# Opening of a fused attention and two-layer feed-forward kernel: pair sums, key copies and three divisions on GpSimd, two chunks of layer one in halves

## The chip, the cores and the metric

The kernel runs on one core of one Trainium2 chip. The metric is the device time of one execution in microseconds (us); lower is better. Work is shared out over five engines, each with its own in-order queue: TensorE (PE in the rows; PEld is its weight load), VectorE (DVE), ScalarE (ACT), GpSimd (POOL) and SyncE (SP), which here issues all DMAs. An engine that waits for a semaphore holds up everything behind the waiting instruction on its own queue.

## The reference

Block-sparse attention over two batches of 768 tokens (8 heads of 64), then two feed-forward layers over the 1536 tokens. Each query sees the 31 tokens around it and 24 summaries, one for each block of 32 tokens: the maximum of the block's keys, the mean of its values.

```python
k_sum = k.reshape(B, H, nb, block, D).max(axis=3)
v_sum = v.reshape(B, H, nb, block, D).mean(axis=3)
scores_l = scale * np.matmul(q, k.transpose(0, 1, 3, 2))
mask_l = np.abs(pos[:, None] - pos[None, :]) < window
scores_s = scale * np.einsum('bhsd,bhnd->bhsn', q, k_sum) + np.log(block)
scores_all = np.concatenate([np.where(mask_l, scores_l, -1e9), scores_s], axis=-1)
a = np.exp(scores_all - np.max(scores_all, axis=-1, keepdims=True))
a = a / (np.sum(a, axis=-1, keepdims=True) + 1e-09)
x = np.matmul(a, np.concatenate([v, v_sum], axis=2))     # then laid out as 1536 x 512
h = np.maximum(x @ w_in, 0.0);  x = h * h @ w_out        # layer one, 512 -> 2048 -> 512
h = x @ w_in2;  out = (h / (1 + np.exp(-h))) @ w_out2    # layer two
```

## The kernel before

Attention goes by 24 tiles of 64 queries, twelve for each batch. A tile's scores are, for each of four pairs of heads (hp), products of its queries with 120 columns: 96 tokens around the tile and the 24 key summaries. Layer one goes by three blocks of 512 tokens, and in each block by 16 chunks of 128 hidden units. A chunk s is one `gemm1` (12 products of 128x512, which fill one accumulator h) and one `gemm2` (12 products). All large products are split in a high and a low part, so three products stand for one.

The first block cannot begin before the first eight tiles, the **lead**, have given 512 rows of x. This is the part that is touched, in `first_block`. Its steps carry short names; of the lead, for tile g and pair hp:

- `kt`, `q`, `vr`, `vl`, `raw`: loads, in this order on SyncE. `kt` is a head pair's keys of a whole batch, `vr` a third of the batch's values, for the means (`vrows`), `vl` the values of four tiles, `raw` a packed weight chunk (`wi` or `wo`).
- `ksum` (VectorE): block maxima of the keys of one pair. `kwl` (ScalarE, 128x384) copies the token columns of four tiles into `kws`, `ksl` (VectorE, 128x96) the summaries beside them; index i is 0 for tiles 0 to 3 and 1 for tiles 4 to 7, so there are eight of each.
- `psl` (TensorE): the scores of one tile and pair, two instructions, read `kws`. `ttl` (VectorE, line 400): mask and minimum. `exl` (ScalarE, line 405): the exponential with its sum.
- `ze`, `rc`, `nt` (VectorE): the guard, the inverse and the four divisions of T. `psa`: transposes on TensorE. `a`: their copy on ScalarE. `av`: product with the values (TensorE). `xh` (ScalarE) and `xl` (VectorE) write the high and the low part of x.
- `vs` (TensorE): the block means of the values, six products of `vrows` with a matrix `share` of 1/32. `vmean` (ScalarE) copies the result, 24x2048, into `vlead` beside the values of tiles 0 to 3 (i = 0) and 4 to 7 (i = 1). `vfm` copies it to two later buffers.
- `sc`, `hi` (ScalarE), `sh`, `st2`, `lo` (VectorE): unpacking and splitting a weight chunk. `relu`, `sq`, `gh` (ScalarE), `gl` (VectorE): between `gemm1` and `gemm2`. `pss`, `ttr`, `exp` and `kwc` are the score steps of the later tiles 8 to 15, which are put in between the chunks.

What sets the order: `first_order` is a list planner. Each step has an engine, a duration, a due time and what it depends on; the planner walks a clock and hands out the steps, and the queues of ScalarE, VectorE, TensorE and SyncE follow its order as it stands (`manual_schedule`). GpSimd is not among these four: where an instruction stands on its queue is settled by the framework, not by the planner. Before, GpSimd has nothing to do in the lead but set small buffers.

Twenty idle products (`turn`, `FILL`) stand on TensorE at the very start and behind the first products of tile 3; they write to a spare accumulator.

## Time and profile before

| | us |
|---|---|
| median of 3 runs (593.97 to 595.03) | 594.18 |
| the profiled execution, its own time | 595.07 |
| its span, first to last instruction | 593.3 |
| busy in the span: PE, DVE, ACT, POOL | 584.0, 388.7, 367.1, 88.9 |
| granted TensorE clock, mean | 0.999 |

Rows of the timeline give the start, the busy time, the engine and line, the operation, what it writes and reads, and how many were merged; on VectorE and ScalarE one instruction's busy time overlaps the next one's start, so what an instruction takes of its queue is the distance of two starts. Idle time before a row stands in brackets with what ended it.

### The profile page before, as it was taken

How to read it: one execution, taken by the hardware profiler on the slowest of the kernel's cores; microseconds unless marked ns; L12 is line 12 of the kernel's file. 1: busy time of each engine (PE TensorE's matmuls, PEld its weight loads, DVE VectorE, ACT ScalarE, POOL GpSimd, SP SyncE). 2: the span in 40 equal slices, each digit the busy share in tenths (PEclk: the TensorE clock that was granted, in tenths of full speed). 3: DMA queues.
4: the chain of work that ended last, by engine and by line, in shares of the span. 5: the costliest groups of instructions: out<-in, count | busy, mean ns of one | idle time of the engine just before them, and what ended most of it. 6: DMA issues, size and time to landing. Idle time of an engine off the chain costs nothing.

```text
span 593.3 us, 9499 instructions
## 1 busy us (share of the span) xinstructions
PE 584.0 (98%) x3300; PEld 491.9 (83%) x3300; DVE 388.7 (66%) x975; ACT 367.1 (62%) x848; POOL 88.9 (15%) x93
## 2 busy tenths in 40 slices
PE   7989999999999999999999999999999999999997
PEld 6578888887887887888888898999988998889995
DVE  5989999733756665267544676777776766666542
ACT  5999998654555655375553676566656655555532
POOL 0000000012554443156333300000000000000000
PEclk9999999999999999999999999999999999999999
DMA  8999999525598888526682112242229411111102
GB/s 308 270 290 352 345 360 339 185 83 181 189 345 303 284 269 303 211 107 206 233 274 68 36 36 89 88 144 88 84 89 378 174 39 36 31 25 35 36 19 106
DMA packets 42240, 104.42 MB, mean 176 GB/s; under 512 B 4560, under 2 KB 11856, under 8 KB 42192
## 3 DMA queue, kind: packets, MB, share of 16 engines
q1 hardware_dynamic: 42192, 103.81, 51.4%
q8 instruction: 26, 0.43, 0.3%
q14 instruction: 22, 0.18, 0.1%
HBM read 78.37 MB, written 25.43 MB: 175 GB/s over the span
## 4 chain that ended last, share of the span: by engine, by line
PE 95%; ACT 2%; DMA 1%; DVE 1%; issue 0%; SPq 0%; DVEq 0%
PE acc L238 45%; PE h L238 23%; PE hx L238 11%; PE hz L238 6%; PE pss L238 4%; PE hy L238 3%; PE psa L442 2%; PE av L238 2%; DMA t_ksum<-in_kT_dram 1%; ACT T L405 1%; PE psv L238 1%; ACT vlead L242 1%; ACT a L242 0%; ACT xt L242 0%; PE idle_out L238 0%; DVE ksum L620 0%
## 5 line engine op out<-in xcount | busy, mean ns | idle before, releaser
L238 PE MATMUL acc<-wq,g 128*128 128x512 f32 x576 | 142.4, 392 | 0.0
L238 PE MATMUL h<-xt,wi 128*128 128x512 f32 x576 | 142.2, 394 | 0.0
L238 PE MATMUL acc<-g,wo 128*128 128x512 f32 x576 | 141.1, 393 | 0.0
L238 PEld LDWEIGHTS acc<-g,wo 128*128 128x128 f32 x576 | 107.1, 188 | 23.1 <-ACT xt L242 0.2
L238 PEld LDWEIGHTS h<-xt,wi 128*128 128x128 f32 x576 | 106.3, 188 | 22.9 <-issue 0.6
L238 PEld LDWEIGHTS acc<-wq,g 128*128 128x128 f32 x576 | 107.1, 188 | 19.7 <-DVE wq L246 0.2
L246 DVE TENSOR_TENSOR g<-r,g 128x512 fp32r<-128x512 f32 x48 | 38.4, 801 | 60.5 <-ACT g L242 31.0
L246 DVE TENSOR_TENSOR r_s<-v,r_s 128x256 fp32r<-128x256 f32 x48 | 20.5, 431 | 50.2 <-ACT r_s L242 50.1
L242 ACT ACTIVATE g<-s 128x384 fp32r<-128x384 f32 x64 | 33.2, 521 | 22.0 <-DVE s L246 22.0
L246 DVE TENSOR_TENSOR g<-s,g 128x384 fp32r<-128x384 f32 x64 | 35.5, 556 | 15.1 <-ACT g L242 13.2
L405 ACT ACTIVATE T<-T,m 128x120 f32<-128x120 f32 x96 | 36.7, 384 | 11.2 <-DVE m L400 11.0
L242 ACT ACTIVATE e<-hx 128x384 f32<-128x384 f32 x32 | 15.7, 492 | 43.8 <-PE hx L238 43.8
L238 PE MATMUL hx<-x_t,r_s 128*128 128x384 f32 x192 | 38.9, 337 | 0.0
L238 PEld LDWEIGHTS hx<-x_t,r_s 128*128 128x128 f32 x192 | 34.5, 188 | 2.7
L932 ACT ACTIVATE s<-e 128x384 f32<-128x384 f32 x48 | 25.2, 525 | 15.4 <-DVE e L246 15.3
L246 DVE TENSOR_TENSOR s<-e,s 128x384 f32<-128x384 f32 x48 | 26.5, 553 | 5.2 <-ACT s L932 5.2
L526 ACT ACTIVATE r<-h 128x512 f32<-128x512 f32 x16 | 9.5, 596 | 30.9 <-PE h L238 30.9
L246 POOL TENSOR_TENSOR wo<-c_wo,wo 128x512 fp32r<-128x512 f32 x16 | 26.1, 1632 | 13.1 <-ACT wo L242 12.6
L242 ACT ACTIVATE r<-u 128x256 fp32r<-128x256 f32 x48 | 19.5, 409 | 12.7 <-PE hx L238 12.7
L243 POOL COPY qd<-qr 128x256 f32<-128x256 f32 x8 | 5.8, 719 | 133.7 <-DVE z L425 125.8
L400 DVE CUSTOM_DVE_ANT_0 T<-pss,cst_sb 128x120 f32<-128x120 f32 x96 | 21.8, 274 | 4.3 <-PE pss L238 4.0
L246 POOL TENSOR_TENSOR r<-r 128x512 f32<-128x512 f32 x16 | 17.0, 1064 | 48.6 <-ACT g L531 48.6
(112 smaller groups left out, 912.0 us busy)
## 6 DMA issues: line engine op xcount, KB each, us to landing
raw_wi<-in_w_in_dram SPq DMA_DIRECT2D x16, 512.0 KB, 5.6
raw_wo<-in_w_out_dram SPq DMA_DIRECT2D x16, 512.0 KB, 5.6
raw_wp<-in_w_out_dram SPq DMA_DIRECT2D x16, 512.0 KB, 5.4
split<-wo SPq DMA_DIRECT2D x16, 512.0 KB, 3.7
raw_wj<-in_w_in_dram SPq DMA_DIRECT2D x16, 512.0 KB, 4.6
wo<-split SPq DMA_DIRECT2D x16, 512.0 KB, 3.4
c<-scr_dram SPq DMA_DIRECT2D x32, 256.0 KB, 2.6
scr_dram<-c_wo SPq DMA_DIRECT2D x16, 256.0 KB, 4.4
```

The source lines that it names most:

```text
L238: pe.matmul(o, l, r, **kw)
L242: return act.activation(out=o, in_=i, func=AF.Copy, scale=scale)
L243: return eng.tensor_copy(out=o, in_=i)
L246: return eng.tensor_tensor(out=o, in0=a, in1=b, op=op)
L400: vec.tensor_tensor_reduce(out=d["T"][:, c], in0=d["ps"][:, c], in1=cst_sb[:, kind * NK:kind * NK + NK], scale=-0.125, scalar=3.0e38, op0= ...
L405: act.activation(out=d["T"][:, c], in_=d["T"][:, c], func=AF.Exp, bias=d["m"][:, c:c + 1], scale=-1.0, accum_out=d["z"][:, c:c + 1])
L442: pe.transpose(ps[0:NK, c], d["T"][:, c], id_sb)
L526: act.activation(out=r, in_=h, func=AF.Relu)
L932: act.activation(out=s, in_=src, func=AF.Sigmoid)
```

## The change

Seven of the eight key copies `kwl` go from ScalarE to GpSimd, and so do all eight summary copies `ksl` from VectorE. The values are loaded so that a partition holds two neighbouring tokens; GpSimd adds the two (`vpair`, 128x512, three of them), and `vs` needs three products instead of six, with a `share` that VectorE now makes from the identity in the constants (`member`). Of the two copies `vmean` the second goes from ScalarE to VectorE; `vfm` goes to GpSimd. The divisions `nt` of tiles 2, 4 and 6 go from VectorE to GpSimd. The first two chunks' `gemm1` are cut in halves of 256 tokens: `half1` reads x of tiles 0 to 3 alone and stands before the last two tiles of the lead on TensorE; the second half follows when all eight are there. Planner durations and due times are changed with it (the diff shows those that come with a moved step), and the weight chunks are taken in another order.

```diff
+NHALF = 2
+NORMS = (2, 4, 6)
...
-            op("act", "kwl", (hp, i), .5, -50 + hp + 51 * i, [("kt", hp, 0)])
-            op("vec", "ksl", (hp, i), .13, -50 + hp + 48 * i, [("ksum", hp, 0)])
-    for c in range(6):
-        op("pe", "vs", c, .92, 2.7 + .1 * c, [("vr", c // 2, 0)])
+            op("pool" if i or hp else "act", "kwl", (hp, i), .5, -50 + hp + 51 * i, [("kt", hp, 0)])
+            op("pool", "ksl", (hp, i), .25, -50 + hp + 48 * i, [("ksum", hp, A)])
+    op("vec", "member", 0, .25, 1.9, [("cst", 0, 0)])
+    for c in range(3):
+        op("pool", "vpair", c, 1.07, -20, [("vr", c, 0)])
+        op("pe", "vs", c, .95, 1.6 + .01 * c, [("vpair", c, A), ("member", 0, A)])
...
-        op("vec", "nt", g, .78, due, [("rc", g, .1)])
+        op("pool" if g in NORMS else "vec", "nt", g, 1.3 if g in NORMS else .78, due, [("rc", g, .1)])
...
+        if s < NHALF:
+            op("pe", "half1", s, 1.45, due - 30, [("xl", g, A) for g in range(NGRP)] + [("lo", ("wi", s), A)])
...
-            sp.dma_start(out=t, in_=vP[0, r0:r0 + 2 * P].rearrange("(c p) d -> p c d", p=P))
+            sp.dma_start(out=t, in_=vP[0, r0:r0 + 2 * P].rearrange("(p c) d -> p c d", p=P))
...
-            copy(act, kws[i][hp // 2][:, hp % 2, :, 0:NWIN], bass.AP(w.tensor, w.offset, [w.ap[0], [QT, NGRP], w.ap[1]]))
+            copy(pool if i or hp else act, kws[i][hp // 2][:, hp % 2, :, 0:NWIN], bass.AP(w.tensor, w.offset, [w.ap[0], [QT, NGRP], w.ap[1]]))
...
-            copy(vec, kws[i][hp // 2][:, hp % 2, :, NWIN:NK], bass.AP(s.tensor, s.offset, [s.ap[0], [0, NGRP], s.ap[1]]))
+            copy(pool, kws[i][hp // 2][:, hp % 2, :, NWIN:NK], bass.AP(s.tensor, s.offset, [s.ap[0], [0, NGRP], s.ap[1]]))
...
+        def member(_):
+            n = 2 * P // KBLK
+            rows = share[:, NSUM - n:NSUM]
+            vec.tensor_reduce(out=rows, in_=id_sb.rearrange("p (n j) -> p n j", n=n), op=ALU.add, axis=AX.X)
+            vec.tensor_scalar(out=rows, in0=rows, scalar1=1.0 / KBLK, scalar2=None, op0=ALU.mult)
+
+        def vpair(c):
+            tt(pool, vrows[c][:, 0], vrows[c][:, 0], vrows[c][:, 1], ALU.add)
+
         def vs(c):
-            lo = NSUM - P // KBLK - c * (P // KBLK)
-            mm(psv[NWIN:NK], share[:, lo:lo + NSUM], vrows[c // 2][:, c % 2], start=(c == 0), stop=(c == S // P - 1))
+            lo = NSUM - (c + 1) * (2 * P // KBLK)
+            mm(psv[NWIN:NK], share[:, lo:lo + NSUM], vrows[c][:, 0], start=(c == 0), stop=(c == S // (2 * P) - 1))
 
         def vmean(i):
             means = psv[NWIN:NK]
-            copy(act, vlead[NWIN:NK, i * NGRP:i * NGRP + NGRP].rearrange("p g h d -> p g (h d)"),
+            copy(vec if i else act, vlead[NWIN:NK, i * NGRP:i * NGRP + NGRP].rearrange("p g h d -> p g (h d)"),
                  bass.AP(means.tensor, means.offset, [means.ap[0], [0, NGRP], means.ap[1]]))
 
         def vfm(i):
-            copy(act, vf[i][NWIN:NK], vlead[NWIN:NK, 0])
+            copy(pool, vf[i][NWIN:NK], vlead[NWIN:NK, 0])
...
+        def half1(s):
+            h = hs[s] = ps_h.tile([P, 512], F32, tag="h", name=f"h0_{s}")
+            gemm1(wi1[s], x, 0, 256, h[:, 0:256])
+
         def gemm1_(s):
-            h = hs[s] = ps_h.tile([P, 512], F32, tag="h", name=f"h0_{s}")
-            gemm1(wi1[s], x, 0, 512, h)
+            if s < NHALF:
+                gemm1(wi1[s], x, 256, 256, hs[s][:, 256:512])
+            else:
+                h = hs[s] = ps_h.tile([P, 512], F32, tag="h", name=f"h0_{s}")
+                gemm1(wi1[s], x, 0, 512, h)
```

How the order moves, at three places. The first is GpSimd's queue in the lead. Before, between the last small buffers and the first work of the second block (`kws` and `t_ksum` don't occur; ISA is an instruction without operands that stands once, ahead of GpSimd's first tensor-tensor operation):

```order
L597 MEMSET t_ksum_2_184 128x16
L356 MEMSET share 32x1 x4
L597 MEMSET t_ksum_3_186 128x16
L243 COPY qd_108<-qr_106 128x256
L246 ISA
L246 TENSOR_TENSOR wo_0_1847<-c_wo_0_1848,wo_0_1847 128x512
```

Now, from the third pair's keys on (`t_ksum_2` and `t_ksum_3` are the keys of pairs 2 and 3, `kws_1` the columns of both, 133 for tiles 0 to 3 and 135 for tiles 4 to 7, `vrows` the values):

```order
L250 COPY kws_1_133<-t_ksum_2_180 128x4x96
L250 COPY kws_1_135<-t_ksum_2_180 128x4x96
L250 COPY kws_1_133<-t_ksum_3_182 128x4x96
L250 COPY kws_1_135<-t_ksum_3_182 128x4x96
L253 ISA
L253 TENSOR_TENSOR vrows_191<-vrows_191 128x512
L250 COPY kws_1_133<-ksum_197 128x4x24
L250 COPY kws_1_135<-ksum_197 128x4x24
L253 TENSOR_TENSOR vrows_193<-vrows_193 128x512
L250 COPY kws_1_133<-ksum_197 128x4x24
L250 COPY kws_1_135<-ksum_197 128x4x24
L253 TENSOR_TENSOR vrows_195<-vrows_195 128x512
```

The ISA instruction has moved from the second block into the lead, and pair 2's summary copies stand behind four key copies and behind the first pair sum, pair 3's behind the second.

The second place is TensorE where layer one begins (`h_0`, `h_1` are the accumulators of the first two chunks). Before:

```order
L238 MATMUL av_549<-a_161,vlead 64x64 x8
L238 MATMUL av_561<-a_166,vlead 64x64 x8
L238 MATMUL av_572<-a_171,vlead 64x64 x8
L238 MATMUL av_584<-a_176,vlead 64x64 x8
L238 MATMUL pss_599<-kw_245,qr_107 64x120 x8
L238 MATMUL h_0_619<-xt_88,wi_462 128x512 x12
L238 MATMUL h_1_653<-xt_88,wi_638 128x512 x12
```

Now, from the product of tile 5 with its values on:

```order
L245 MATMUL av_527<-a_162,vlead 64x64 x8
L245 MATMUL h_0_539<-xt_88,wi_498 128x256 x12
L447 MATMUL psa_571<-cst_sb,T_166 120x128 x4
L447 MATMUL psa_580<-cst_sb,T_171 120x128 x4
L245 MATMUL av_594<-a_167,vlead 64x64 x8
L245 MATMUL av_607<-a_172,vlead 64x64 x8
L245 MATMUL h_1_626<-xt_88,wi_604 128x256 x12
L245 MATMUL h_0_539<-xt_88,wi_498 128x256 x12
L245 MATMUL h_1_626<-xt_88,wi_604 128x256 x12
L245 MATMUL h_2_693<-xt_88,wi_659 128x512 x12
```

A half of each of the first two chunks stands ahead of the lead's end, and the later tile's score product `pss` that stood ahead of `h_0` has gone further back.

The third place is TensorE at tile 12 (`psv` is the batch's value summaries). Before:

```order
L238 MATMUL pss_1480<-kw_1113,qr_106 64x120 x8
L238 MATMUL pss_1496<-kw_1265,qr_107 64x120 x8
L238 MATMUL acc_0_703<-g_10_1440,wo_1210 128x512 x3
L238 MATMUL acc_1_704<-g_10_1440,wo_1210 128x512 x3
L238 MATMUL acc_2_705<-g_10_1440,wo_1210 128x512 x3
L238 MATMUL acc_3_706<-g_10_1440,wo_1210 128x512 x3
L238 MATMUL h_12_1561<-xt_88,wi_1338 128x512 x12
L442 MATMUL psa_1581<-cst_sb,T_1510 120x128 x4
```

Now:

```order
L245 MATMUL pss_1522<-kw_1127,qr_106 64x120 x8
L245 MATMUL pss_1535<-kw_1266,qr_107 64x120 x8
L245 MATMUL h_12_1560<-xt_88,wi_1329 128x512 x12
L447 MATMUL psa_1596<-cst_sb,T_1547 120x128 x4
L245 MATMUL acc_0_719<-g_11_1507,wo_1354 128x512 x3
```

The `gemm2` that stood between tile 12's scores and its transposes has gone ahead of the scores.

## Rows read from the trace of the kernel before

**Rows 1.** Busy by stretch: us, PE, PEld, DVE, ACT, POOL (instructions), PEclk, DMA share, GB/s.

```profile
15.20:37.40 22.20, 19.97 (x247) 13.03 (x245) 18.74 (x105) 21.81 (x72) 0.00 (x0) 1.00 1.02 273
37.40:145.90 108.50, 108.50 (x676) 87.02 (x674) 85.79 (x253) 83.99 (x194) 3.96 (x4) 1.00 0.78 268
589.40:591.50 2.10, 0.02 (x1) 0.00 (x0) 0.69 (x1) 0.00 (x0) 0.00 (x0) 1.00 0.54 204
591.60:593.30 1.70, 0.00 (x0) 0.00 (x0) 0.00 (x0) 0.00 (x0) 0.00 (x0) 0.50 0.09 34
```

**Rows 2.** The chain that ended last, in order of time: start us, us, what.

```profile
28.99 3.63 ACT vlead L242 x2
...
36.22 1.22 PE pss L238 x16
37.44 5.67 PE h L238 x24
```

**Rows 3.** The first load of values on SyncE: duration, start, landing.

```profile
L612 SPq DMA_DIRECT2D vrows<-in_vP_dram x1: 835/835/835, 4.1 to 4.1; - x1
...
DMA to landing us min/median/max: 9.6/9.6/9.6
```

**Rows 4.** Timeline of TensorE and VectorE in the lead: products of pair 2, block means, divisions.

```profile
12.49 4.03 PE L238 MATMUL pss<-kws,qrlead 64*64 64x120 f32 x60
...
24.35 1.90 PE L238 MATMUL psv<-vrows,share 128*24 128x512 f32 x4
24.71 0.85 DVE L436 TENSOR_SCALAR T<-T,r 128x120 f32<-128x120 f32 x4
```

**Rows 5.** Timeline of GpSimd and VectorE where GpSimd first adds.

```profile
127.13 0.63 POOL L243 COPY qd<-qr 128x256 f32<-128x256 f32 x1 [125.50 <-DVE z L425]
127.31 1.10 DVE L436 TENSOR_SCALAR T<-T,r 128x120 f32<-128x120 f32 x4
132.63 1.39 POOL L246 TENSOR_TENSOR wo<-c_wo,wo 128x512 fp32r<-128x512 f32 x1 [4.87 <-ACT wo L242]
150.87 1.04 POOL L246 TENSOR_TENSOR r<-r 128x512 f32<-128x512 f32 x1 [3.77 <-ACT g L531]
```

**Rows 6.** Timeline of ScalarE in the lead.

```profile
10.49 0.51 ACT L242 ACTIVATE kws<-t_ksum 128x384 f32<-128x384 f32 x1
...
24.45 0.60 ACT L242 ACTIVATE a<-psa 120x512 f32<-120x512 f32 x1
24.95 0.39 ACT L405 ACTIVATE T<-T,m 128x120 f32<-128x120 f32 x1
25.32 0.62 ACT L242 ACTIVATE wi<-c_wi 128x512 fp32r<-128x512 f32 x1
25.84 0.38 ACT L405 ACTIVATE T<-T,m 128x120 f32<-128x120 f32 x1
32.65 0.94 ACT L242 ACTIVATE xt<-av 128x256 fp32r<-128x256 f32 x3
```

**Rows 7.** Timeline of VectorE around the start of layer one.

```profile
36.14 0.69 DVE L293 SCALAR_TENSOR_TENSOR c_wo<-c_wo,raw_wo 128x512 int32<-128x512 int32 x1
36.75 0.75 DVE L246 TENSOR_TENSOR xt<-av,xt 128x256 fp32r<-128x256 f32 x2
37.42 0.68 DVE L293 SCALAR_TENSOR_TENSOR c_wi<-c_wi,raw_wi 128x512 int32<-128x512 int32 x1
41.03 0.42 DVE L290 TENSOR_SCALAR raw_wo<-raw_wo 128x512 int32<-128x512 int32 x1
41.37 0.27 DVE L400 CUSTOM_DVE_ANT_0 T<-pss,cst_sb 128x120 f32<-128x120 f32 x1
```

**Rows 8.** Tiles 12 and 13: score products, the next keys' load and its landing.

```profile
107.17 2.18 PE L238 MATMUL pss<-kw,qr 64*64 64x120 f32 x32
108.74 0.39 SPq L366 DMA_DIRECT2D kw<-in_kW_dram  x1
DMA to landing us min/median/max: 2.8/2.8/2.8
```

More of the change, by code (lines that the diff above doesn't have):

```diff
@@ L137, in first_order @@
         op("vec", "xl", g, .36, due, [("xh", g, A)])
-    chunks = [(x, s) for s in range(NF) for x in ("wi", "wo")]
+    chunks = sorted(((x, s) for s in range(NF) for x in ("wi", "wo")), key=lambda c: c[1] + 1.5 * (c[0] == "wo"))
     for i, (x, s) in enumerate(chunks):
@@ L157, in first_order @@
         due = chunk_due(s)
-        op("pe", "gemm1", s, 2.72, due, [("xl", g, A) for g in range(NLEAD)] + [("lo", ("wi", s), A)] +
-           [("relu", s - 2, A)] * (s >= 2))
+        if s < NHALF:
+            op("pe", "half1", s, 1.45, due - 30, [("xl", g, A) for g in range(NGRP)] + [("lo", ("wi", s), A)])
+        op("pe", "gemm1", s, 1.45 if s < NHALF else 2.72, due, [("xl", g, A) for g in range(NLEAD)] + [("lo", ("wi", s), A)] +
+           [("half1", s, 0)] * (s < NHALF) + [("relu", s - 2, A)] * (s >= 2))
         op("act", "relu", s, .57, due, [("gemm1", s, M)] + [("gl", s - 2, A)] * (s >= 2))
@@ L354 @@
     pool.memset(share, 0.0)
-    for j in range(P // KBLK):
-        pool.memset(share[j * KBLK:(j + 1) * KBLK, NSUM - P // KBLK + j:NSUM - P // KBLK + j + 1], 1.0 / KBLK)
     st = {}
@@ L734, in xh @@
             x_high(g)
-        do = dict(kt=kt, q=q, cst=cst_, vr=vr, vl=vl, ksum=ksum_, kwl=kwl, ksl=ksl, vs=vs, vmean=vmean, vfm=vfm, kv=kv, kvr=kvr,
+        do = dict(kt=kt, q=q, cst=cst_, vr=vr, vl=vl, ksum=ksum_, kwl=kwl, ksl=ksl, member=member, vpair=vpair, vs=vs, vmean=vmean, vfm=vfm, kv=kv, kvr=kvr,
                   vend=vend, vendc=vendc, vfc=vfc, kw=kw_load, qr=q_load, vf=v_load, kwc=k_sums,
                   pss=scores, ttr=minima, exp=exps, ze=guard, rc=inverse, psl=psl, ttl=lambda a: minimum(*a),
-                  exl=lambda a: exponential(*a), nt=lambda g: norm(g, vec),
+                  exl=lambda a: exponential(*a), nt=lambda g: norm(g, pool if g in NORMS else vec),
                   psa=transposes, a=a_copy, av=products, xh=xh, xl=x_low, raw=raw, sc=sc,
                   sh=lambda xs: dec_low(name(xs)),
-                  st2=lambda xs: dec_join(name(xs), cs[xs]), scr=scr_, hi=hi, lo=lo, gemm1=gemm1_, relu=relu, sq=sq, gh=gh,
+                  st2=lambda xs: dec_join(name(xs), cs[xs]), scr=scr_, hi=hi, lo=lo, half1=half1, gemm1=gemm1_, relu=relu, sq=sq, gh=gh,
                   gl=gl, gemm2=gemm2_)
```

21 lines of the change are left out of this document (11 added, 10 removed).

## The prediction

> **What bounds the kernel now.** I first read the busy time by stretch. From 37.4 us on, TensorE is busy in all of the 108.50 us of the first stretch after the lead, at the full clock, while VectorE and ScalarE are at some 80%; its last product ends at 589.4 [rows 1]. So the end is set by two numbers: when layer one starts, and how much TensorE work is left then. In the 22.2 us before, ScalarE is busy for 21.81, TensorE for 19.97, VectorE for 18.74, GpSimd not at all [rows 1]: the lead is bound by ScalarE, with 0.4 us left over. The chain of waits says the same: it runs through the two copies `vmean` on ScalarE (3.63 us, so 1.8 each), then 1.22 us of the score products `pss`, then the first two chunks `gemm1`, 5.67 us together, 2.8 each or 2.72 without their gap [rows 2]. An idea that takes 3 us of copies from ScalarE therefore aims at the right engine. What is to be settled is what the lead waits for afterwards.
>
> **The start of pair 2 (a new wait).** GpSimd's queue is not in the planner's order. In it the summary copies of pair 2 stand behind pair sum 0, which needs the first values. These were issued at 4.1 and landed 9.6 us later, at 13.7 [rows 3]. Before, nothing waited for them this early: pair 2's products began at 12.49 [rows 4]. Now: pair sum 0 starts at 13.7 and takes 1.04 to 1.39 (GpSimd's two additions of 128x512); I take 1.1, nearer to the second, which is a steady one, than to the first one after an ISA instruction [rows 5]. So 14.8. The two summary copies of 96 elements each are bounded by GpSimd's copy of 256 elements in 0.63 [rows 5]: 0.24 each in proportion, hardly under 0.13 (the planner's figure for VectorE). The first must end and be seen by TensorE, then the products run: 15.2, for 15.0 to 15.6. That is 2.7 us later than before, and since all three engines take their instructions in order, the other tiles' steps stand behind it. ScalarE starts again about 0.7 us later (two products, the mask), at 15.9.
>
> GpSimd's four key copies of pairs 2 and 3 stand ahead of pair sum 0. ScalarE could copy pair 2's first at 10.49 without waiting [rows 6], so the keys were there. At 0.63 (the 256 elements) to 0.95 (1.5 times that) they take 2.5 to 3.8 us, and end between 13.0 and 14.3; the wait for the values covers them at 0.8 each (13.7), and at the upper end they add 0.6.
>
> **ScalarE and VectorE from there.** ScalarE then has 26 of its 32 exponentials (six of pairs 0 and 1 stand ahead in its queue) by 0.38 (the distance of two starts is 0.37 without a neighbour's wait), that is 9.9; six copies `a` by 0.50, 3.0; one `vmean`, 1.8; one `sc` and one `hi`, 1.1 (0.52 for a `hi`); six `xh` by 0.28 to 0.31, 1.7 [rows 2, 6]. The sum is 17.5; with the same 0.4 of gaps as before the last exponential ends at 33.8. The seven key copies and a `vmean` are gone from it, 0.51 and 1.8 each by row [rows 2, 6], and the wait has eaten what that brought.
>
> VectorE is next. Behind the last exponential it has guard and inverse (0.25) and tile 7's divisions, 0.85 by row [rows 4]: 34.9. Then ten steps stand in its queue ahead of the last `xl`, or are it: one `sh` 0.34, two `st2` 1.22, two `sh` 0.68, a small copy 0.13, two `lo` 1.2, two `xl` 0.68, durations by the distances of starts (`st2` 36.14 to 36.75, `xl` 0.67 for two, `sh` 41.03 to 41.37) [rows 7]; 4.25 in all, so 39.15, and the second halves begin at **39.3**. By ScalarE alone (tile 7's transposes, copy, products, `xh`) it would be 37.9. The lead's end was 37.44: **+1.86**.
>
> **The halves.** A half costs 1.36. Both first halves stand ahead of the lead's end, at about 31.5 and 38.0, where TensorE has room: its lead work between 15.2 and 39.3 is some 17.7 of 24.1 us. So 2.72 us of layer one are done when the second halves start: **-2.72**. If the second of them found no gap, half of this would go. Of two moved products, the `pss` of 1.22 us [rows 2], which stood ahead of layer one, now runs behind: **+1.22**, since TensorE is full there.
>
> **Tile 12.** TensorE now runs into `psa` of tile 12 with one `gemm1` between scores and transposes, where a `gemm2` stood too. The scores end at about 108.3 before, the keys' load follows at 108.74 and lands 2.8 later [rows 8], then copy and divisions, so about 4.3 us from the scores' end (X) in the worst case, against 3.8 of cover: **+0.3**, bounds 0 and 0.8.
>
> **The clock.** While pair 2 is late, TensorE has little to do for 3 to 4 us. In the trace the granted clock was 1.00 (2.4 GHz) up to 591.5 and 0.50 (1.2 GHz) from 591.6 on, with TensorE idle since 589.4 [rows 1]. If it falls here, the products that ScalarE waits for first, 4.03 us for 60 or 0.067 each [rows 4], take twice that: eight of them add 0.5. I take **+0.2**, bounds 0 and 0.6.
>
> **Costed at nothing.** The divisions on GpSimd: 1.0 to 1.2 by its rows for 512 elements [rows 5], up to 2.1 hidden, since tile 6's scores end four exponentials (1.5 us) ahead of tile 7's and VectorE's own took 0.85; without the cover +0.6. `vs`: three products fewer of 0.47 each (1.90 for four) [rows 4], in TensorE's idle time. The second `vmean` on VectorE: up to 2.7 (2048 elements at `xl`'s 0.335 for 256 [rows 7]), beside ScalarE's exponentials; it would cost as much if `av` of tile 4 came to wait for it, but several tiles' work lies ahead. `vfm`, `member`, the small buffers: nobody waits.
>
> **The sum.** +1.86 - 2.72 + 1.22 + 0.3 + 0.2 = +0.86, say +0.9. The profiled execution took 595.07, so 595.97; it is 0.89 above the median of 594.18, so the forecast is **595.1**. What a measurement of this kernel can tell from no change is about 0.2%, 1.2 us: up to 593.0 is faster, from 595.4 slower. The forecast lies inside, near the upper edge.
>
> **Rivals.**
> (a) *The lead ends earlier than I walk it.* VectorE's ten steps need not stand in a row: those of the weights may run in its waits while ScalarE is the slower. Then the second halves start at ScalarE's 37.9, 1.4 us earlier: 593.7. Without the terms of the clock and of tile 12: 593.2. If the values, whose pieces in DRAM are now two tokens long and not one, land 1 us earlier, 592.3. For it: ScalarE, not VectorE, was the full engine [rows 1]. Against: `st2` and `xl` were close together at the lead's end before [rows 7]. Chance 0.33, of which 0.24 under 593.0.
>
> (b) *GpSimd's first addition starts late.* In front of it stands an ISA instruction without operands, now in the lead. GpSimd was idle for 4.87 us ahead of its first addition; the trace puts the end of that down to ScalarE's copy of `wo` [rows 5]. So what ISA costs by itself is between 0 and 4.87. Before pair sum 0 GpSimd has up to 1.1 us of spare time if its key copies are quick; a cost above that delays everything behind. 2.5 us would give +1.4, 596.5; 4.87 would move pair sum 0 from 12.6 to 17.5, +3.8, 598.9. This is the case that ends clearly slower; it decides from 1.1 us up. I give it 0.13, since the row has another reason for the wait.
> The Trainium skill, page "GPSIMD Engine Reference", section 2.1 "Instruction dispatch", says that the first call to a freshly loaded GpSimd function costs about 6 us that no instruction shows. By it pair sum 0 would come near 18.6 and the time near 600, an estimate from that page. The trace's 4.87 us speaks against so much, if that load happens here at all.
>
> (c) *GpSimd and VectorE slow each other.* A group of four divisions on VectorE took 0.85 alone [rows 4] and 1.10 where GpSimd's copy ran beside it [rows 5]. GpSimd now has some 7 us of work in the second part of the lead; if a third of it meets VectorE's long operations at this rate, 0.29 us for each us, with VectorE setting the end, and GpSimd's summary copies and divisions stretched as well, that is about +1.0: 596.1. Chance 0.12.
> The Trainium skill, page "Perfetto Trace Analysis", section "Optimizing Scalar/DVE Operations", says that the two share a read port, so that moving work from one to the other might not help. By that rule the copies `ksl` and the divisions bring VectorE less than their time; the trace agrees, by the 1.10 against 0.85.
>
> **How the numbers follow.** The forecast's own case has 0.42: 0.27 within 0.2%, and 0.15 above it, when the tile 12 and clock terms or the key copies come out at their upper ends (+0.5, +0.4, +0.6). Rival (a) has 0.24 faster and 0.09 same, (b) 0.13 and (c) 0.12 slower. Together: faster 0.24, same 0.36, slower 0.40. The range goes from (a) with all its parts, 592.3, to just under (b) at its upper end, 598.4.
>
> **What would show it.** In the trace after: pair sum 0 starts at 13.7, straight after its load (at 17.5 in case (b), with an idle GpSimd and landed values); the first product of pair 2 at 15.2; ScalarE idle before 15.9; the first halves at about 31.5 and 38.0 and the second from 39.3 (37.9 in (a)); a gap of 0.3 on TensorE at tile 12; the granted clock below 1.00 or not around 15 us; divisions of 1.1 and over on VectorE beside GpSimd's work (c). The forecast is wrong if pair 2 starts before 14.5, or if the second halves start outside 38.5 to 40.

## The result: slower by 6.2 us

| | before | after |
|---|---|---|
| median of four runs, us | 594.44 (593.97 to 595.03) | 600.88 (599.96 to 601.19) |
| profiled execution, its own time and span, us | 595.07, 593.3 | 601.19, 599.3 |
| granted TensorE clock, mean | 0.999 | 0.991 |

The ratio is 1.0105, with an interval of 1.0088 to 1.0123: 6.2 us of 594.4, 5.2 to 7.3. The forecast was 595.1, and the time lies above its range.

TensorE's timeline of the changed kernel in the lead (start us, busy us, engine, line, operation, what it writes and reads, shape, count, and in brackets the idle time before and what ended it) shows where it is late:

```profile
14.31 4.72 PE L245 MATMUL pss<-kws,qrlead 64*64 64x120 f32 x44 [3.13 <-POOL kws L250]
19.52 2.58 PE L245 MATMUL pss<-kws,qrlead 64*64 64x120 f32 x36 [0.49 <-DVE m L405]
22.04 0.65 PE L447 MATMUL psa<-cst_sb,T 128*120 128x128 f32 x4
...
31.80 1.62 PE L245 MATMUL av<-a,vlead 120*64 120x64 f32 x48 [1.83 <-ACT vlead L249]
...
36.13 1.70 PE L245 MATMUL h<-xt,wi 128*128 128x256 f32 x12
38.43 0.33 PE L447 MATMUL psa<-cst_sb,T 128*120 128x128 f32 x1 [0.60 <-POOL T L441]
...
43.06 2.13 PE L245 MATMUL h<-xt,wi 128*128 128x256 f32 x12
```

Pair 2 begins at 14.31 (12.49 before, [rows 4]), the first half at 36.13, the other at 43.06. That one finds no room: behind it the second halves begin at 43.06 + 2.13 = 45.19, where `gemm1` before began at 37.44 [rows 2]. From there on nothing changes any more. By stretch (us, PE busy, instructions, PEclk, DMA share, GB/s), answers of the changed kernel, those of the first block for TensorE alone, show the clock and that TensorE is full afterwards:

```profile
13.00:14.00 1.00, 0.00 (x0) 0.66 1.05 418
14.00:20.00 6.00, 5.20 (x50) 0.50 1.06 258
20.00:22.00 2.00, 2.00 (x34) 0.96 1.05 226
...
42.00:44.00 2.00, 2.00 (x26) 0.50 0.78 186
```

```profile
46.00:150.00 104.00, 104.00 (x677) 84.22 (x676) 81.71 (x246) 78.90 (x186) 3.93 (x4) 1.00 0.76 262
```

So the forecast's own sum, made with the measured start, comes out: 45.19 - 37.44 = 7.75, less 2.72 for the halves, plus 1.22 for the moved `pss`, is 6.25; the two profiled executions lie 6.12 apart. There is no gap at tile 12 (104.00 busy of 104.00). Everything that went wrong is in one term, the start of the second halves: 45.19 and not 39.3.

ScalarE's timeline of the changed kernel has these rows with an idle time ahead between its restart and the last exponential; the last row here is that exponential:

```profile
15.37 0.40 ACT L410 ACTIVATE T<-T,m 128x120 f32<-128x120 f32 x1 [4.01 <-DVE m L405]
...
20.56 0.39 ACT L410 ACTIVATE T<-T,m 128x120 f32<-128x120 f32 x1 [0.66 <-DVE m L405]
...
22.73 0.60 ACT L249 ACTIVATE a<-psa 120x512 f32<-120x512 f32 x1 [1.68 <-PE psa L447]
...
29.87 1.87 ACT L249 ACTIVATE vlead<-psv 24x2048 f32<-24x2048 f32 x1 [2.33 <-DVE vlead L250]
...
38.04 0.38 ACT L410 ACTIVATE T<-T,m 128x120 f32<-128x120 f32 x1
```

It ends at 38.42, where the forecast had 33.8, although it restarted at 15.37 and not at 15.9. The three idle times make 4.67 us; the forecast had allowed 0.4. VectorE's timeline of the changed kernel has its copy of the value means, tile 7's divisions, and the end of its work for the lead:

```profile
27.54 2.30 DVE L250 COPY vlead<-psv 24x2048 f32<-24x2048 f32 x1
...
38.98 0.97 DVE L441 TENSOR_SCALAR T<-T,r 128x120 f32<-128x120 f32 x4
...
42.28 0.68 DVE L253 TENSOR_TENSOR wi<-c_wi,wi 128x512 fp32r<-128x512 f32 x1
...
43.87 0.42 DVE L253 TENSOR_TENSOR xt<-av,xt 128x256 fp32r<-128x256 f32 x1
```

GpSimd's timeline of the changed kernel:

```profile
12.79 1.26 POOL L253 TENSOR_TENSOR vrows<-vrows 128x512 f32<-128x512 f32 x1 [1.76 <-DMA vrows<-in_vP_dram]
14.00 0.47 POOL L250 COPY kws<-ksum 128x96 f32<-128x96 f32 x2
...
23.27 4.72 POOL L441 TENSOR_SCALAR T<-T,r 128x120 f32<-128x120 f32 x8 [5.87 <-DVE z L430]
...
37.79 2.30 POOL L441 TENSOR_SCALAR T<-T,r 128x120 f32<-128x120 f32 x4 [4.75 <-DVE r L433]
```

The first pair sum starts straight on its values; they landed at 12.7, a microsecond earlier than before [rows 3]. A tile's four divisions take 2.3 us on GpSimd, where the forecast had 1.0 to 1.2, up to 2.1, and 0.85 on VectorE [rows 4].

### The profile page after: what moved, and what is told of

Read it like the earlier page. It is cut to its first block, busy times and chain, and to the rows that moved or that the text cites. A ratio compares the mean times of both kernels' runs of the same rounds, so it can differ in the third digit from the quotient of the medians.

```text
span 599.3 us, 9537 instructions
## 1 busy us (share of the span) xinstructions
PE 585.7 (98%) x3318; PEld 495.4 (83%) x3318; DVE 392.4 (65%) x958; ACT 361.9 (60%) x838; POOL 105.4 (18%) x121
## 4 chain that ended last, share of the span: by engine, by line
PE 94%; ACT 2%; DMA 1%; DVE 1%; POOL 1%; SPq 1%; issue 0%; DVEq 0%; POOLq 0%
PE acc L245 44%; PE h L245 22%; PE hx L245 11%; PE hz L245 6%; PE pss L245 4%; PE hy L245 3%; PE av L245 2%; DMA vrows<-in_vP_dram 1%; PE psa L447 1%; ACT T L410 1%; ACT a L249 0%; POOL T L441 0%; DVE vlead L250 0%; ACT vlead L249 0%; SPq L605 0%; ACT xt L249 0%
## 5 line engine op out<-in xcount | busy, mean ns | idle before, releaser
L245 PE MATMUL h<-xt,wi 128*128 128x512 f32 (+1 forms) x600 | 143.2, 387 | 0.0
L245 PEld LDWEIGHTS h<-xt,wi 128*128 128x128 f32 x600 | 107.9, 189 | 22.2 <-issue 0.6
L253 DVE TENSOR_TENSOR g<-r,g 128x512 fp32r<-128x512 f32 x48 | 37.1, 774 | 59.4 <-ACT g L249 30.3
L253 POOL TENSOR_TENSOR wo<-c_wo,wo 128x512 fp32r<-128x512 f32 x16 | 27.7, 1729 | 12.6 <-ACT wo L249 12.2
L249 ACT ACTIVATE r<-u 128x256 fp32r<-128x256 f32 x48 | 19.5, 409 | 14.0 <-PE hx L245 12.7
L249 ACT ACTIVATE a<-psa 120x512 f32<-120x512 f32 x24 | 14.1, 593 | 15.9 <-PE psa L447 15.9
```

Source lines behind the costliest of these rows:

```text
L245: pe.matmul(o, l, r, **kw)
L249: return act.activation(out=o, in_=i, func=AF.Copy, scale=scale)
L253: return eng.tensor_tensor(out=o, in0=a, in1=b, op=op)
```

## Experiments

Ratios are to the kernel before, run on the same chip in the same job, with their interval; microseconds after them are the part of that ratio above 1, times 594.4. The changed kernel stands at 1.0105, +6.2. One thousandth is 0.6 us; where two intervals overlap, as they do for every single part that was taken back except the halves, the difference of the two figures is only an indication, and what the part did is read from the rows. The rows are those of one execution of a run, its figure is the median of several. In a run "in the kept order" only the engine of a step is changed and the written order is that of the kernel it starts from; "planned anew" means that the planner's input was changed too.

### One part of the change taken back

**Summary copies back on VectorE** (kept order).

```diff
-            copy(pool, kws[i][hp // 2][:, hp % 2, :, NWIN:NK], ...
+            copy(vec, kws[i][hp // 2][:, hp % 2, :, NWIN:NK], ...
```

> The eight summary copies stand on VectorE again, in the same written order; all else as in the changed kernel. Theory A (the pair sum ahead of them on GpSimd, waiting for the values until 12.79 us, starts the loss): pair 2's products begin near 12.5 instead of 14.31, TensorE's idle time there is under 2 us, the granted clock stays at or near 1.00 between 14 and 20 us, and the time falls by 2 to 3.5, to 597.4 to 598.9. Rival B (the start is caught up again, the loss is made by the bank wait and the divisions later): the start moves, the second halves still begin within 1 us of 45.2, and the time stays within 1 of 600.9.

Measured: 1.0084 (1.0061 to 1.0108), +5.0; 1.2 taken back, within the intervals. The chain did move: pair 2 begins at 12.6, the second of the first halves at 39.83 (43.06). But VectorE's last summary copy now stands beside GpSimd's pair sum, and the clock falls later instead. VectorE's timeline, then stretches (PE, PEld, DVE, ACT, POOL, PEclk, DMA share, GB/s) of this run:

```profile
12.65 0.20 DVE L250 COPY kws<-ksum 128x96 f32<-128x96 f32 x1
12.97 1.16 DVE L250 COPY kws<-ksum 128x96 f32<-128x96 f32 x1
```

```profile
38.00:40.00 2.00, 2.00 (x33) 1.88 (x34) 2.00 (x6) 1.79 (x5) 0.00 (x0) 0.50 0.56 106
```

The same copy takes 0.20 and 1.16 us. Theory A holds for the mechanism; its size came out under the expected 2 to 3.5.

**Value means in two banks.**

```diff
-            mm(psv[NWIN:NK], share[:, lo:lo + NSUM], vrows[c][:, 0], ...
+            for ps in (psv, psw[0]):
+                mm(ps[NWIN:NK], share[:, lo:lo + NSUM], vrows[c][:, 0], ...
...
-            means = psv[NWIN:NK]
+            means = (psw[0] if i else psv)[NWIN:NK]
```

> The value means are made twice, into two banks (three products more on TensorE), so that ScalarE and VectorE read one each. Theory B (the second reader of one bank waits for the first): ScalarE's copy starts at about 27.5 and not at 29.87, its idle 2.33 us is gone, the last exponential ends about 2 us before 38.3, and the time falls by 1.5 to 2.3, to 598.6 to 599.4. Rival: the wait is only an order that the data needs, or TensorE's transposes and the divisions on GpSimd end last anyway: the time stays within 0.5 of 600.9.

Measured: 1.0102 (1.0056 to 1.0148), no gain. The wait itself is gone, as ScalarE's and VectorE's timelines of this run show:

```profile
28.83 1.87 ACT L249 ACTIVATE vlead<-psv 24x2048 f32<-24x2048 f32 x1
```

```profile
29.61 2.30 DVE L250 COPY vlead<-psw 24x2048 f32<-24x2048 f32 x1 [1.48 <-PE psw L245]
```

The two copies overlap; so it was the shared accumulator. But TensorE made three products of 1 us (two instructions each) more ahead of them, and the products with the values begin at 31.67 against 31.80. Still the first `gemm2` begins 1.0 us earlier (49.64, against 50.66), and this execution loses that again at tile 12. VectorE's and TensorE's timelines there:

```profile
120.97 0.21 DVE L250 COPY kw<-ksum 128x96 f32<-128x96 f32 x1 [1.15 <-DMA kw<-in_kW_dram]
```

```profile
121.52 0.81 PE L447 MATMUL psa<-cst_sb,T 128*120 128x128 f32 x4 [1.36 <-DVE T L441]
```

The divisions stand on VectorE behind that copy, and the copy waits for the next keys, which landed 4.7 us after their issue (2.9 and 3.9 in the changed kernel). It is the wait that the prediction had sized at 0.3. The run shows the cause of the wait for the means, and not its price.

**Both value-mean copies on ScalarE** (kept order, the first four tiles' first).

```diff
-            copy(vec if i else act, vlead[NWIN:NK, i * NGRP:i * NGRP + NGRP]...
+            i = 1 - i
+            copy(act, vlead[NWIN:NK, i * NGRP:i * NGRP + NGRP]...
```

> Both value-mean copies on ScalarE, the one for tiles 0 to 3 first, in the written order of the changed kernel; nothing else is moved and TensorE gets no product more. Theory B (the two readers of one bank run one after the other, and that costs): the first copy runs from about 27.5 to 29.4, the products with the values begin at 29.4 instead of 31.80, ScalarE is free of both at 31.1 instead of 31.74, VectorE has 2.3 us less to do, and the time falls by 0.6 to 2, to 598.9 to 600.3. Rival (what comes behind, the division of tile 6 on GpSimd and the late start of pair 2, sets the end): within 0.4 of 600.9.

Measured: 1.0085 (1.0051 to 1.0120), +5.1; 1.1 taken back, by the ratio inside the expectation, but within the intervals. Both copies run from 27.43 to 31.06, and the products begin at 29.94, 1.9 earlier.

**Divisions back on VectorE** (kept order): `norm(g, vec)` for all tiles.

> The divisions of tiles 2, 4 and 6 stand on VectorE again, in the same written order. Theory C (a tile's division takes 2.36 us on GpSimd and tile 6's is on the path to the last transposes): the transposes of tiles 6 and 7 end about 1 us before 41.1 and the time falls by 0.7 to 1.5, to 599.4 to 600.2. Rival (VectorE is the scarcer engine, three times 0.85 us more there cost as much as they bring): within 0.5 of 600.9.

Measured: 1.0117 (1.0076 to 1.0159), not better. ScalarE's wait for VectorE's mean copy grew from 2.33 to 3.2 us: VectorE has two more divisions, of tiles 2 and 4, ahead of that copy, 1.7 us. The theory falls for this surrounding: what the divisions cost on GpSimd they cost on VectorE too.

**Ten idle products in TensorE's wait.** `FILL` of pair 1 at tile 3 is 14 instead of 4.

> The changed kernel with ten more idle products on TensorE behind the last products of pair 1, where it stood idle for 3.13 us. Theory D (that idle time brings the clock to half until 20.1, and the products at half clock cost time beyond the wait): the granted clock stays above 0.95 from 13 to 20 us, the first 44 products of pair 2 take about 3.0 us and not 4.72, and the time falls by 0.7 to 1.5, to 599.4 to 600.2. Rival (ScalarE's exponentials set the pace there whatever the clock): within 0.5 of 600.9.

Measured: 1.0086 (1.0055 to 1.0118), +5.1; 1.1 taken back, as theory D had it, though within the intervals. TensorE's timeline and its stretches in this run, against 4.72 us for 44 products and 0.50 above, then a later stretch of all engines:

```profile
16.45 1.94 PE L245 MATMUL pss<-kws,qrlead 64*64 64x120 f32 x28 [0.42 <-POOL kws L250]
```

```profile
13.00:14.00 1.00, 0.79 (x4) 1.00 1.01 397
14.00:20.00 6.00, 4.29 (x62) 1.00 1.05 262
```

```profile
32.00:34.00 2.00, 2.00 (x44) 2.00 (x41) 2.00 (x9) 2.00 (x6) 0.23 (x1) 0.50 0.90 214
```

0.069 us a product and 0.107 before: the idle time costs a second time, by the clock at 1.2 instead of 2.4 GHz. The clock then falls at another place, behind the wait for the value means. And ScalarE's wait for the first transposes stays, although the clock is full:

```profile
21.91 0.60 ACT L249 ACTIVATE a<-psa 120x512 f32<-120x512 f32 x1 [1.45 <-PE psa L447]
```

**No halves.** `NHALF = 0`.

> The first two chunks are whole again (the order is planned anew behind the lead). If the halves bring what was forecast (2.72 us of layer one ahead of the lead's end) less the 0.9 us by which the second of them now runs into the lead's end, the time rises by 1.5 to 2, to 602.4 to 602.9. Rival (the halves delay the lead's last products, which stand behind them, by as much as they save): within 0.5 of 600.9 or faster.

Measured: 1.0190 (1.0149 to 1.0231), +11.3, so 5.1 slower than the changed kernel, far over the expected 1.5 to 2. TensorE's stretches in this run:

```profile
36.00:38.00 2.00, 0.07 (x4) 1.00 0.02 8
38.00:50.00 12.00, 10.73 (x56) 0.57 0.61 210
```

Without a half to run, TensorE is idle for 2 us ahead of tile 6's transposes, and then works at a mean clock of 0.57 for 12 us. So in the changed kernel the halves seem to save more as a filler than as work done early, which is 2.72 us at most. This is read from the rows; the order behind the lead was planned anew in this run as well.

### Several parts taken back

**Three parts, planned anew**: summary copies and divisions on VectorE, both mean copies on ScalarE, in the planner's input as well.

> Summary copies on VectorE, both value-mean copies on ScalarE, all divisions on VectorE, and the order planned anew with that; the key copies on GpSimd, the pair sums, three products and the halves stay. Theory (the late start of pair 2, the two readers of one bank one after the other, and the 2.3 us division of tile 6 make the loss together; each alone is covered by the other two): the second halves begin before 39.5 instead of 45.2 and the time falls by 5.5 to 7.5, to 593.4 to 595.4. Rival (halves, pair sums or key copies cost by themselves): it stays above 597.

Measured: 1.0092 (1.0060 to 1.0124), +5.5, far above what was expected. The new plan was at fault as well: the matrix for the means (`member`, due behind all eight tiles' scores) went from an early place in VectorE's queue (9.04 us in the changed kernel) to 28.71 us, and the means' products with it. VectorE's timeline of this run:

```profile
13.05 1.25 DVE L250 COPY kws<-ksum 128x96 f32<-128x96 f32 x1
...
16.77 1.28 DVE L430 TENSOR_SCALAR z<-z 128x4 f32<-128x4 f32 x1
...
28.71 0.28 DVE L653 TENSOR_REDUCE share<-cst_sb 128x8 f32<-128x128 f32 x1
```

The first two rows are steps of 0.2 us; that they took over a microsecond beside GpSimd's pair sums is why these were priced alone, further down.

**The same with the second mean copy on GpSimd**, from the first copy's result.

> As the run with the three parts back, but the second value-mean copy on GpSimd, from the first one's result in the main memory of the core instead of the accumulator bank. If ScalarE still bounds the lead (1.85 us less on it): 0.5 to 1.8 below that run, 592 to 594. If GpSimd takes over 4 us for the 2048 elements, tiles 4 to 7 wait for it and the time is equal to that run or up to 1.5 above.

Measured: 1.0119 (1.0080 to 1.0158), +7.1: tile 4's products wait 1.42 us more for GpSimd, the second of the expected outcomes.

**Three parts in the kept order.**

> The three together in the written order of the changed kernel, unlike the run that planned it anew: summary copies and divisions on VectorE, both value-mean copies on ScalarE. Theory (late pair 2, one bank for two readers and slow divisions cover one another, and make most of the loss only together): pair 2 begins near 12.6, the second halves begin at 39 to 40.5 instead of 45.2, and the time falls by 4 to 5.5, to 595.4 to 596.9. Rival (the written order itself, which counts on steps that take less, or the weights' landing is what costs): it stays above 598.

Measured: 1.0049 (1.0031 to 1.0067), +2.9: 3.3 taken back, clear of the intervals, and by the ratio a little less than the theory's 4 to 5.5. In the profiled execution (597.04 us) the clock is 1.00 throughout the lead. That does not hold for all ten: three with a mean clock of 0.999 or 1.000 took 595.72 to 598.41, the other seven, at 0.991 to 0.997, took 597.82 to 599.25. So a part of what remains seems to be lost by the clock still. ScalarE's timeline of before has its last exponential here, and the mean copies behind it, from 28.99 [rows 2]:

```profile
28.49 0.38 ACT L405 ACTIVATE T<-T,m 128x120 f32<-128x120 f32 x1
```

In this run ScalarE's timeline has:

```profile
24.95 3.63 ACT L249 ACTIVATE vlead<-psv 24x2048 f32<-24x2048 f32 x2
...
31.59 0.42 ACT L410 ACTIVATE T<-T,m 128x120 f32<-128x120 f32 x1
...
34.82 0.38 ACT L410 ACTIVATE T<-T,m 128x120 f32<-128x120 f32 x1
```

The written order puts the mean copies ahead of the last seven exponentials; these end at 35.2, six microseconds later than before, and tile 7's divisions, transposes and products come after that. VectorE's timeline of this run gives a second reason:

```profile
36.52 0.42 DVE L297 TENSOR_SCALAR raw_wo<-raw_wo 128x512 int32<-128x512 int32 x1
...
40.38 0.42 DVE L253 TENSOR_TENSOR xt<-av,xt 128x256 fp32r<-128x256 f32 x1
```

Between tile 7's divisions and the last low part of x, from 36.52 on, it has seven steps for weight chunks and a small copy to do. Five of them are of the third chunk and later ones, whose unpacking the change holds back until tile 7's divisions are done in its plan (a dependency `held`, which the kernel before does not have). Both are readings of the rows; neither was isolated.

**The same with six products and no pair sums.**

```diff
         def vpair(c):
-            tt(pool, vrows[c][:, 0], vrows[c][:, 0], vrows[c][:, 1], ALU.add)
+            pass
```

> As the run with the three together in the kept order, but without pair sums: six products for the value means, in the place of the three. Theory E: VectorE's steps of over 1 us between 12 and 18 us are gone, pair 2 and 3 come 0.5 to 1 us earlier, against 1.3 us more of products on TensorE; the time falls by 0.3 to 1.2, to 1.003 to 1.0044 of the kernel before (1.0049 in that run). Rival (TensorE's 1.3 us count in full): it rises by 0.5 to 1.3, to 1.0057 to 1.007.

Measured: 1.0057 (1.0038 to 1.0076), the same within the intervals. The scores of all tiles but the last end 1.5 us earlier (36 products from 15.48, against 17.02), as the theory said; then, in the profiled execution (599.67, the slowest of four), TensorE waits 2.05 us for VectorE's low parts of x, its clock is 0.50 from 34 to 38, and it waits 1.40 us more at tile 12, for keys that again landed 4.7 us after their issue. Two of the other executions took 597.75 and 598.10 at a mean clock of 1.000, so the clock is not what takes the gain away in all of them; what does stays open.

**Planned anew with measured durations**: 2.36 us for a division on GpSimd (tile 2 alone), 1.27 for a pair sum, the second mean copy behind the first, summary copies on VectorE, `member` first.

> The changed kernel with summary copies on VectorE, the share matrix made first, GpSimd dividing tile 2 alone, and the order planned anew by what the traces show: 2.36 us for a division on GpSimd, 1.27 for a pair sum, the second value-mean copy behind the first. Theory F (the written order counts on steps that take less, so the queues stand still in turn): the first half begins before 32, the second halves at 38 to 39.5, and the time is 594 to 596.5 (1.000 to 1.003 of the kernel before). Rival (the order is not it: ScalarE's freed time is simply not where the lead needs it): not below the run with the three together, 1.0045 or more.

Measured: 1.0042 (1.0027 to 1.0056), +2.5. The first half begins at 32.70. A plan with the right prices is, within the intervals, no better than the three parts taken back, as the rival had it.

### Each part alone, on the kernel before

**Key copies** on GpSimd (planned anew).

> The kernel before with the seven key copies alone moved from ScalarE to GpSimd, 0.46 us each, 3.2 together. If ScalarE is what bounds the lead of before and its time comes back in full: 591.0 to 592; if VectorE or the value means are next after 0.5 to 1.5: 592.7 to 593.7; if the means' products and copies set the end whatever ScalarE has before them: within 0.4 of 594.2.

Measured: 0.9996 (0.9975 to 1.0016): nothing. **Key copies and second mean copy** (kept order of the kernel before):

```diff
-            copy(act, kws[i][hp // 2][:, hp % 2, :, 0:NWIN], ...
+            copy(pool if i or hp else act, kws[i][hp // 2][:, hp % 2, :, 0:NWIN], ...
...
-            copy(act, vlead[NWIN:NK, i * NGRP:i * NGRP + NGRP]...
+            copy(vec if i else act, vlead[NWIN:NK, i * NGRP:i * NGRP + NGRP]...
```

> The kernel before, in its own order, with the key copies on GpSimd and the second value-mean copy on VectorE: 5 us less on ScalarE, which was busy for 21.8 of 22.2 us. If the lead were bound by ScalarE's work: 2 to 4 below the kernel before. If the order and what lands when set the lead's end, as the runs so far say: within 0.6 of it.

Measured: 1.0021 (1.0012 to 1.0030), +1.2, although ScalarE has 5 us less to do. ScalarE's and VectorE's timelines of this run show what is next:

```profile
24.18 0.69 ACT L285 ACTIVATE c_wi<-raw_wi 128x512 f32<-128x512 f32 x1 [1.35 <-DMA raw_wi<-in_w_in_dram]
32.30 1.32 ACT L242 ACTIVATE xt<-av 128x256 fp32r<-128x256 f32 x3 [1.03 <-PE av L238]
```

```profile
24.18 0.43 DVE L290 TENSOR_SCALAR raw_wi<-raw_wi 128x512 int32<-128x512 int32 x1 [1.50 <-DMA raw_wi<-in_w_in_dram]
...
31.31 2.30 DVE L243 COPY vlead<-psv 24x2048 f32<-24x2048 f32 x1
```

Both engines arrive early at the first weight chunk, which stands in their queues ahead of other tiles' work, and wait until it lands at 24.2. And VectorE's mean copy keeps all low parts of x waiting until 33.6. This execution (596.46) is the slowest of its ten, whose median is 595.28; how long the others waited for the weights is not known.

**Second mean copy alone.**

> The kernel before, in its own order, with the second value-mean copy alone on VectorE. It begins when the first ends (one bank): about 30.8 to 33.1. ScalarE can write the high parts of tiles 0 to 3 from 31.7 instead of 32.65, but VectorE's low parts wait until 33.1 and tiles 4 to 7 as well. Theory B (a second reader that waits is worth nothing): within 0.5 of the kernel before. If ScalarE alone sets the lead's end: 0.7 to 1.5 below.

Measured: 1.0010 (0.9999 to 1.0020), +0.6: nothing gained, as theory B had it, and its bound of 0.5 lies inside the interval.

**Divisions of tiles 2, 4 and 6 alone.**

> The kernel before, in its own written order, with the divisions of tiles 2, 4 and 6 on GpSimd and nothing else moved. If a division on GpSimd (2.36 us against 0.85) delays its tile's transposes, and those the tiles behind: 0.7 to 2.5 above the kernel before of this job. If VectorE's freed 2.5 us are worth as much: within 0.5 of it, or up to 0.7 below.

Measured: 1.0025 (1.0003 to 1.0048), +1.5. A division takes 2.32 to 2.55 us there, and TensorE begins layer one's products at 38.59 and not 37.44.

**Halves alone.**

> The kernel before with the first two chunks in halves and nothing else moved. Its lead is as long as it was; TensorE has 2.2 us idle in it, most of it before the last products with the values. By the forecast's term (a half is worth 1.36 where TensorE has room) one half fits: 592.8 to 593.6. If it stands in the way of the last tiles' products by as much as it brings: within 0.4 of 594.3; if the halves cost more than the whole (their weight loads): up to 595.3.

Measured: 1.0020 (0.9998 to 1.0042), +1.2, at best unchanged: the half finds its place (34.81), and tile 7's products stand behind it. The term of 1.36 a half is worth nothing where it delays what the lead waits for.

**Pair sums alone**: three additions on GpSimd whose results nobody reads.

```diff
         def vs(c):
+            if c % 2 == 0:
+                tt(pool, idle_in, vrows[c // 2][:, 0], vrows[c // 2][:, 1], ALU.add)
```

> The kernel before with three additions of 128x512 more on GpSimd, of the values as they land; nobody waits for their results, and no other engine's order changes. Theory E (VectorE's plain copies and small divisions stand still while GpSimd adds: 1.25 and 1.28 us for steps of 0.2 us in a run above): VectorE has two or three steps of over 1 us between 13 and 19 us, layer one begins 0.5 to 1.5 us later than 37.44, and the time rises by 0.4 to 1.5 over the kernel before of this job. Rival (VectorE's steps there are masks, which do not stand still, or it makes up for it before the lead ends): within 0.3 of the kernel before.

Measured: 1.0037 (1.0023 to 1.0052), +2.2, above the expected 0.4 to 1.5, although no engine waits for these results. GpSimd's and VectorE's timelines of this run:

```profile
13.21 2.62 POOL L246 TENSOR_TENSOR idle_in<-vrows 128x512 fp32r<-128x512 f32 x2 [11.58 <-DVE m L400]
16.54 1.28 POOL L246 TENSOR_TENSOR idle_in<-vrows 128x512 fp32r<-128x512 f32 x1 [0.71 <-DMA vrows<-in_vP_dram]
```

```profile
14.46 0.28 DVE L400 CUSTOM_DVE_ANT_0 T<-pss,cst_sb 128x120 f32<-128x120 f32 x1
14.67 1.19 DVE L425 TENSOR_SCALAR z<-z 128x4 f32<-128x4 f32 x1
...
16.23 1.86 DVE L436 TENSOR_SCALAR T<-T,r 128x120 f32<-128x120 f32 x4
```

The masks run beside the additions at 0.28. A division's guard of 128x4, 0.17 us elsewhere, lasts 1.19, to the end of the second addition; the four divisions 1.86 against 0.85, with the third addition in them. TensorE begins layer one's products at 38.66.

**Keys, halves, six early products, mean copies on two engines, later weights**, planned anew from the kernel before, as the best that the parts seemed to allow.

> From the kernel before: key copies on GpSimd, halves, the value means' six products placed early, the second value-mean copy on VectorE behind the first, weights in the changed kernel's order and kept back behind the lead's divisions; no pair sums, and nothing but key copies on GpSimd. If ScalarE's freed time is what the lead needs and the weights no longer stand in front of it: 592.5 to 594. If the loads' landing or VectorE is next: 594 to 596.

Measured: 1.0027 (1.0010 to 1.0045), +1.6: the second outcome. No version run here beats the kernel before.

## Why the prediction was wrong, point by point

**The start of pair 2** was right in its mechanism: GpSimd's queue held the summary copies behind pair sum 0, and that behind the values. The size was a little high (14.31 against 15.2, and so under the 14.5 that the text itself had named as a sign of being wrong), since the values landed earlier. The key copies cost nothing, at 0.5 us each. Taken back, it is worth 1.2 us, within the intervals.

**ScalarE from there** is the step that failed. Its work was sized well (23.05 us from 15.37 to 38.42, less the gaps, is 18.4, against 17.5), but "the same 0.4 of gaps as before" was carried over from an order in which the engines had been matched. The gaps were 4.67. They are most of the error in the start of the second halves, 45.19 against 39.3: 4.3 by the gaps, 0.9 by the work, 0.5 by VectorE's tail, 0.9 by the half that ran in between, less 0.5 by the earlier restart; the rest is rounding. The gaps have three sources.

- *First*, 2.33 of them are VectorE's copy of the same accumulator bank: the second reader waits for the first. The prediction costed the second `vmean` at nothing "beside ScalarE's exponentials". The rule was to be had: the Trainium skill, page "PSUM — Partial Sum Buffer", section "PSUM bank collisions raise a hardware error", says that the compiler's scheduler makes two engines that touch the same bank in the same 32 partitions wait for each other, reads included; the trace agrees (29.87, behind 27.54 + 2.30), and the run with two banks shows it gone.
- *Second*, 1.68 are the wait for TensorE's first transposes, which stand behind 36 score products (19.52 to 22.10); before, they stood among them (the first at 16.45). With the idle products, at full clock, this wait is still 1.45, so most of it comes from the written order.
- *Third*, 0.66 come behind products at half the clock; with the idle products they are gone.

**The clock** had been taken at +0.2, with 0 and 0.6 as bounds, for eight products; it was half from 14 to 20, for all 44 products that had waited, and half again from 42 to 44, where the second of the first halves ran (2.13 us instead of 1.36). The idle products price the first of these at 1.1 us, within the intervals.

**Costed at nothing: the divisions on GpSimd.** The price was taken from one instruction of 512 elements, 1.04 to 1.39; four instructions of 120 elements take 0.58 each. Tile 6's division (37.79 to 40.09) ends 0.14 us after tile 7's on VectorE (38.98 + 0.97), and TensorE's transposes of both stand in order behind it. "Up to 2.1 hidden" was an estimate of cover that the later exponentials no longer gave. Alone on the kernel before it costs 1.5 us (0.2 to 2.9), and taken back alone it brings nothing: VectorE works without a gap from tile 7's divisions to its last `xl`, so in the changed kernel it sets the end, and not those transposes.

**VectorE's tail**, 5.35 from the last exponential to the last `xl`, measured 5.87 (38.42 to 44.29), close. **The halves**: 2.72 held as an amount, but the second of them did not fit, as the text had feared; it stood 0.9 us in front of the second halves, 0.77 of that by the clock. It could hardly have run earlier, since VectorE wrote the low part of its weights only by 42.96 (42.28 + 0.68). **Tile 12**: 0 and not 0.3 in the changed kernel's trace; the wait that was meant is real, 1.36 and 1.40 us in two of the runs above.

**Rival (b)**, a late first addition, did not happen: the idle time ahead of it ends with the values' landing, and the 4.87 us in [rows 5] were ScalarE's copy and nothing else. By the rule of the Trainium skill, page "GPSIMD Engine Reference", section 2.1 "Instruction dispatch", the time would have come near 600, and it did, for other reasons; the 6 us it states are shown by no run here, since the changed kernel's first addition starts with its data (12.79, after 1.76 us of idle time). **Rival (c)** had the right pair of engines, the wrong law: it spread 0.29 us over each shared microsecond, where the rows show single steps held to the end of an addition. The Trainium skill, page "SBUF — State Buffer", section "SBUF: two separate sides", says that the port pair which the two share is locked for a whole instruction, on VectorE's side for some of its operations only, and that the loser stands still; the trace agrees, with 1.19 for a step of 0.17 and 0.28 for a mask. Of the changed kernel's own loss this explains little, as VectorE was idle or at masks during its pair sums; it may be a part of why taking pair 2's delay back brings 1.2 and not 2 to 3.5.

**Rival (a)** and the whole sum rested on [rows 1], ScalarE busy for 21.81 of 22.2. That row is true, and the conclusion is not: with 5 us less on ScalarE the kernel gets no faster. In the rows of that run the first weight chunk's landing, VectorE and the order of the tiles are all within a microsecond or two of it; which of them would come next in a faster execution is not shown.

By parts, alone on the kernel before: keys -0.2, second mean copy +0.6, halves +1.2, divisions +1.5, pair sums +2.2. That is 5.3 together, near the 6.2 measured, but that is luck: each has an interval of 0.6 to 1.3 us to either side, pair sums and halves act otherwise in the changed kernel, and the summary copies, the other order of the weight chunks and their holding back were not tried alone. What is shown is that pair 2, the bank and the divisions together make 3.3 us. What stays open is the 2.5 to 2.9 us that remain when they are put right. From the rows, three things lie there: the mean copies ahead of the last exponentials, the weight steps held until behind tile 7's divisions, and the clock in most executions. In the run with the three parts in the kept order ScalarE's last `xh` ends at 39.3 and VectorE's last `xl` at 40.8, so I estimate the second at up to 1.1 us, 40.8 less 39.3 and 0.4 for the `xl` itself. None was tried by itself.

## What to carry to other kernels

A busy share of 98% says that an engine is full, not that the others have room: before counting a saved microsecond, look for what lands or ends within the next one, in queue order. When work goes to a second engine, look for what the two then share, an accumulator bank or a port, and price small instructions by an instruction of that size. An idle time of TensorE can be paid twice, by the wait and by the clock behind it, as the 3.13 us here were; the 1.83 us at 30 us in the same execution were not. A filler, even idle products, can take the second payment back, but look where the clock falls next.

## What the runs showed of the hardware

- VectorE's plain copies and scalar steps stand still while GpSimd adds two operands: 0.20 to 1.16, 0.17 to 1.19 and 1.28 us. Masks with an accumulator in the same stretch stayed at 0.28.
- Two engines that copied from one accumulator bank ran one after the other (2.33 us of waiting); with the result in two banks the copies overlapped.
- GpSimd's `tensor_scalar` of 128x120 takes 0.58 us, VectorE's 0.21; a copy of 128x384 takes 0.5 on either GpSimd or ScalarE.
- Behind TensorE's idle time of 3.13 us its granted clock was 0.50 (1.2 GHz) from 14 to 20 us, though it was busy for 5.20 of these 6.
- Values whose pieces in DRAM were two tokens long landed in 8.7 us instead of 9.6, but the pieces are not shown to be the reason: over all runs the first load took 7.9 to 9.1 us with them and 8.8 to 9.6 without.
- The load of the next keys at tile 12 landed 2.9 and 3.9 us after its issue in the changed kernel, and 4.7 us in two runs that differ from it in the lead alone.
